# Inverse factors loaded on ScalarE's queue, first loads and last inverse in halves, and a new order, in a two-stage attention and gated spectral convolution kernel

## The chip, the cores and the metric

One core of one Trainium2 chip. The time is the device time of one execution in microseconds, the median of five runs. A profiled execution gives a page and a trace; its span runs from the first to the last instruction and is a little shorter than the time.

The engines are TensorE (PE in the profile, PEld for its weight loads), VectorE (DVE), ScalarE (ACT), GpSimd (POOL) and SyncE (SP). SP, ACT and POOL issue DMAs, each on a queue of its own.

## The reference

Eight batches, eight heads, 576 positions, head dimension 64. A packed attention makes 32 rows per head from p, k and v; a second attention lets q look at these 32 rows. The result, laid out as 576 x 512 per batch, is projected three ways; the middle third is convolved along the sequence (by Fourier transform) with a filter, gated by the other two thirds, and projected out.

```python
def sm_attn(qq, kk, vv):
    s = scale * np.matmul(qq, kk.transpose(0, 1, 3, 2))
    ...
    return np.matmul(a, vv)
p_packed = sm_attn(p, k, v)
out = sm_attn(q, p_packed, p_packed)
...
proj = x @ w_proj
x1, x2, x3 = ...
X2 = np.fft.rfft(x2, n=S, axis=1)
H = np.fft.rfft(filter_fft, n=S, axis=0)[None, :, :]
x2_conv = np.fft.irfft(X2 * H, n=S, axis=1)
y = x1 * x2_conv * x3
return (y @ w_out).astype(np.float32)
```

## The kernel before

The Fourier transforms are matrix products with constant factors: wc and wt for the forward transform, ac for the inverse. The second attention is never multiplied out: its weights a2 (per position and packed row) are transformed or transposed themselves, and the packed rows, held in R, are first multiplied with w_proj (tile wp), giving qm. So most of the work is matmuls of 16-bit tiles with 128 x 128 weights.

Each batch passes through four stages, written as generators:

- front (line 706): transposes k (k_turn, PSUM tile kTp), first scores s1 and their exponentials e1, the products with v and the sums (pv), the normalised packed rows ppn, their transpose ppT and its four copies into R (ppk in the profile), q's transposes (q_turn, copied to qT: heads 0 to 3 by VectorE, 4 to 7 by ScalarE), second scores (s2, s2t), exponentials e2 and the normalised weights a2n.
- turn (line 872): qm from R and the thirds of wp; the forward transform fp of the weights, giving fa; transposes a2tp giving a2t.
- middle (line 937): the spectrum f, multiplied by the filter's spectrum (tiles tt, gm), and the gate w from the products x1 and x3.
- back (line 1004): the inverse x2 (the matmuls `x_b<-ac,gm` in the profile, since all of x1, x2 and x3 carry the short name x_b), y as the product of gate and inverse, and five output projections o (three row groups of 128, one of mixed rows, and one, for odd batches, of the rest of two batches; tile os), each evicted and written out.

Batches 0 to 7 run as a pipeline: front of batch b beside turn of b−1, middle of b−2 and back of b−3. Ahead of it a prologue transforms the filter (hp).

Inputs are loaded by `load(b)` on POOL's queue: kn, vn and qn, cast to 16 bits on the way, in two buffers each. The first loads are those of batch 0, then the three thirds of wp, then ac, then batch 1, then wout. ac holds four factor matrices of 128 x 576; the fourth, negated values of the first two, is used for batch 0 alone (APART), whose four combinations gm aren't formed beforehand. In later batches (TURNED, KEYS, FLIP) SP turns q, k and the weights with transposing DMAs instead of PE.

The order of the instructions isn't the order of the code. A Recorder collects all operations; a planner (`schedule`) plays them through a model of engines, queues and buffers and issues, on each engine, the ready operation with the lowest priority number. The numbers are decoded from the long string PRIORITY: one shift for each of the 3168 operations. The planned order is fixed as each engine's program order. Where the planner's PE has nothing ready in the first 34 us it adds spin matmuls, whose result is unused. The planner's durations and queue constants (`hold`, `transfer_ns`, SLOW) act on the order only.

For the last batch each output projection is made in two halves of 256 columns, the first evicted by ScalarE, the second by VectorE, and half of some writes go out on ScalarE's queue.

Of the kernel before, what the change touches and what calls it, by code (L numbers as in the profile page):

```python
# [14 lines left out]
FP16 = mybir.dt.float16  # L15
# [4 lines left out]
P = 128  # L20
# [23 lines left out]
def _constants(S):  # L44
# [37 lines left out]
    ac = _f16(np.stack([*inv, np.where(COLUMN_T % 2 == 0, -inv[1], -inv[0])]).transpose(1, 0, 2))  # L82
# [4 lines left out]
    'c-oy-2RxN+8$ZuEMoLCSBqSoqmKCxq$1Ege%gPMN-Xmm0_RP)}iYVE#3W<sc8S$z&Q8?%MoPE&y`@Z+Po-^*}y6@}0{@1*3f587`q5+rudu2{1'  # L87
    '8~O8>?SK{W-z*%YoO~+%Tt%^qQ}W9U2RlaHGHLgJl$x5MTjnE|O=tXmbA`*LWsEs{+0(W2u5F=3<VZLF^xH>q4MinR3hA+#L$2=GUWVuNsrK=('
    'P?H64>q|+UKWnSXPlIHbwCnrUz3>H84Ekhorn#g_O|LykA@SxMO{a^7*i8=VRcVk5*jOEYF{Kve?CYLpb+yu2k?}gE`7^}VDcHP&v97D5g`1Jl'
    'HEm@FTSaqAEn`Dfc?Ctdq@<PvTu??*l}}Av@dCfvWmOFsEir*WO#@9axr_5UHlexow*(;f!h!>W+@!#fy-Gg%<0>f!!z{!}=7*d=(+Z4h(%UJo'  # L90
    '1TNEt^!E4kcSm<u29r?H{vsVCg}{_5XU9kHd;8=)3!dKd?TsHpO;mJ}-=kiV2Qlrj5)3!lHcNDm(BJka+r#_m*3fK8M)K@??|{Z9D#BE3G|<R>'
    '%%f|w91psiJ1H~9PFyxYn(CGmXt+7v&Gqx>Dy=VbwfWc=InKss!X#>GYohugqqXPdGFxMBRX;a3Gl{e?Z8syMtXl<>Xm#&#2iaA{KIB?iN&P}Y'
    '2B>YGW3OY{__V93Vf1IqY;D!E)|y|nl^r#GovrhgS=o(Eh2M%d8^0D8RW`jIO!)phCg(|AW{22}s`#DS53W<u&si4!Iy`LJ5<WnAejrF@;^)ET'
    'Z^x+)uJkW`9-gCsY_!NhzW)-8W^ftkQC5@sfym|ASN_RbM5ShAVCc;Tm4qCeRa$A|Qlulh5u4U23ukAtysU!svdrAH+*)KQWzA~!JioZMu!Sv;'
    'xrPPbpikFy!MpL%=h^M$)P_YlR!OFa^w5I9+Jvszg{Go`+2QwUoy(VKtWMbkSO(f8I)vE?Ojgw~Oi)p4ULc)*9r;DIac1`E(pXBAi=YCx)SOmG'
    'VysK>QUTr65Z&gF<!WvP0T#8j10&UoZ9fB2$djY{Y8qaa2-;09NlL$G`t(%sOO<rv<445^_mP1IHtMm#ul^bdoA%%k);%k|k4&DCU0jV_L4aFa'
    '_88Mqj#C0Bj*5#Mq2}j2%5(Z83zhKxgF<vHM-H7v0_^NG^ibwwl)zDFX*UJu!5;6dCF^7s1LN_%dTZ*+qAAx*`6vrRr8hDM!@|n>Ha?OMjZl+w'
    'P``zOXVv{#J}(Y#-lqP1{cCNQl@@(_jH$f2M*~ld*vAO}g!o%RXJ^LWjP?%q4ZrGZ>1*z4?s}nn?*#Y8rgCCl*2kZo9HPfs%7$vX>kZxsEN&W&'
    'Q?j0*=KR6c_;jSTx!_CGapO;RX*a5Frq~tU4+j9)*c$(yv!d;^)U=>%b65dW&h&Goj<nzk{<VGUo8D~$&CeevL8Cn?e4RaXzb8c&+`3_SQ%KX_'
    'wYIf8ZUTl_Kx!^MnH`w@{B3by#PEv4>>g6n&~RUmxZBsSy109}`iC0F_yt(`>gan$7}(r0Ft}@B?eDJPA*XNcaL32T-PXzN7mb^-tg5NlxpaXB'  # L100
    'dq-;@E0e=sj>?@S$#ta%>f4jD((=6DnQY`}`yCKZyzNuusV>39-jrKxP*T+QxY(gF!a6U*qqO>#T>mA<dvHBd7Dakt87a6P$FRPQ<29G6yEK`}'
    'hdXnt>-s;o-Eg?yDyA!GB%;f&$KcH9$ml|EIXUtG;w^RSteVG#R5^AoeFuK|3r6O9^+j)97IL?WjRKt{FH;|&<Dg)BtpJyiInTFr$5=n&Q966+'
    '^zT%aIn_zJ*Wy#UG0!R{2HJflD4iZh<;IXPbuw#D$w22MoNb;ewsg<bl$OJJM8nd(UaJdhsziuANDI&7FayeqUe>>k>S!6u;Nsa&i~O?w8TQxU'
    '%%_2tbcxFd7&Q!B|3yK~%*{YWx%W7X`Y87y%Bj<&fA1HeAZJ{lUt-+9J~lr|GR=GdgwpTRhp5ShU*g}G<X`MQl3%jfnpd@v?^jh8pYXco5?hfD'
    'MO<dEUHRsd)~LW_lhW|;3VV@R0n0a4x#cfXJL=k>S2nsO6qi?~*EbYBRF{0(o!4Urx6{&q-@X;<;cLvqB0y`Q=X+iHE~%MiW@MasSM}4xzs|=~'
    '96GjdfL3(Au47=bYpnmX#*gyO{4=RVVTlgPretd?C8R~0*@!YkBwxBj)R{Pb#8o*rJ`vV+VKVKDkpWPxpFg<fp`<IU@0qA*znfirXr)=G827lS'
    'xNXv#oBN`M^tCW4N!=@Y1xb3Ie$Jbr%Pt?>R(!hqMn`Mj&knXCm)2Gw$s0D7ju}c(9}oUMZxmoTT;I~wQW2KZ)jseo#6pw@M#5?;4-W~n_?>JY'
    'a63NBD99)EO=^8(_>B7~-|>}&!P%MOg1oaz%Emfeib`@9^$aB>IYgMX*{+*i(L5!~by-M8#++S6LHU5XxPU6>6}n3|s8#suLm4=ILNtbc3PI^t'
    'PZq|#7z+5AU*xG{yc`-*QyKK|FLEKz6tUy{ha|Zq5Bmir#7D`_P9?4lri84B-Vdutj7<=BDe$^y?W$tTMMkT3-A&d^!v9_jh3YY*JMo`%wN>QV'
    'IXh)!4>_OUmXV+zT72?_YV7xq!#XdXv=-FLBRgaN=7-4Ixmx=~O-ZM=oS5VBk&TnOz^fyhELC(VO5Y)KSW|5Cllmgd+SP_@!ptm3g-(}7D|xf$'  # L110
    'r$)^Kqsg9|qsz)yB`kQkR3qWyE;fTT=|780U#&E=(I~Rn#rv-Zw)W2Ve*Vz)PFVAC{bH|ILF!H8t4tzK!b&sB%3ZUA?1Q4cGD<4rQtt$Y=al;8'
    'hZyQ7+o;+{)kJs)KhAE*4twx2`bI|T{i)|QJu8d-tL=3HhiSjCE2tPbR`ELcTKmcB>#N@Kf@@o<b(s233r2psU)DeQYsDZ$0HFU4BVAyiI{B*J'
    '$lhvI>^Sot9&s}Z-76h#H_4#6f!6U!eK)Q&)#k(XjCn6=$nQU8c+S`RQPr85^)|;nE&-uoRpHr2QNC4t2jM0i6ZP&d?w`|Pd2cRoTFB;nTjB7i'
    '-@>Cb$2PaXr`egE6Q2Xsyw54a*#&1h7wP*|V~@q~q(}v~D>o?RD%J?{aOqSf?R!aitjI~?9{J)pIpX^(=2GZ7E2K<PK*B)P(py<w%g|F?%It=P'
    'wSl#nx=yFdg3Kx-D{X38ep_w$!jWHOqhu7DX%we*nAl#jOrEJ#?jTc<vk!dm1}<`NZEs6NbaX^?N@7e<erAwYV_E*A`*kfrg-?s@{i^H}no{Bu'
    '{gT})b9_^?eV;$ePs;PGr=-ZQdh!C%zlUwVpbDP`%PBblH99Rdg>ylU?Uj$;zb;a+S2C1V(lLX3I@!KmBlpSip1V6S`{KjNM-g>y8JcI5_d;vC'
    ')**9Ig=w+Rvbx?3_A&G~jz1a-`c~po7!@q>ab|vEkY-`A;=H1atelIZm1k4Ivu6XHZ{M~ilAg+$q^DtB-FHQtU6A`c&-{KVjbCDxfn75V!+p=v'
    '`nn4TD?+-PU$gw~%qnj$INIJ6?&DTu;U5zbnwwSERv6WCg|Sr=k&y00Q{3C07t>na&{$AkU7l-KsaO%5<J9#rH{0A)(BtNfu%Vv*rir&bjbF>F'
    'R(>O$DdKIjlB!>(KlaY8;lF2_<C1WrBD%uMNI?700TK9Q`QVc_zU7*M>l+pM*)avNArWh1+}}si?<Kldmj>T@R#N$Jo#LY2#Q>MPUVM39S2C#S'
# [1049 lines left out]
```

## Time and profile before

| | |
|---|---|
| time, median of 5 runs | 189.68 us (189.06 to 189.86) |
| profiled execution | 189.66 us, span 187.9 us |
| PE busy | 175.2 us (93%), 2477 matmuls |
| VectorE busy | 143.3 us (76%) |
| ScalarE busy | 123.5 us (66%) |
| GpSimd busy | 137.7 us (73%) |
| POOL's load queue | 17.11 MB; medians of 11.6 to 17.7 us from issue to landing |
| SP's queue | 14.59 MB |
| granted TensorE clock | 0.999 |

Almost all lines of the page name L538, the line of the Recorder that calls every recorded operation, so groups are told apart by tile names. The page's slices show PE full from the second slice to the last but one, and the DMA engines full for the first 27 of 40 slices. The batches can't be told apart by name in the page; the trace's times tell them.

### The profile page before, as it was taken

What the parts mean: (1) busy time and instruction counts of PE and PEld (TensorE: products, weight loads), DVE (VectorE), ACT (ScalarE), POOL (GpSimd) and SP (SyncE); (2) the same over time, 40 slices, a digit from 0 to 9 for tenths busy, and PEclk for the clock granted to TensorE, in tenths of its full rate; (3) what the DMA queues carried; (4) which work ended last, traced back from release to release, by engine and by line L of the source; (5) the groups of instructions that cost most, each with busy time, mean ns of one, the idle gap of its engine ahead of it and who ended that gap; (6) DMA issues with size and microseconds to landing.
All of it is one profiled execution on the core that took longest, in us unless ns stands there. A gap on an engine that the chain in (4) does not pass through costs nothing.

```text
span 187.9 us, 5930 instructions
## 1 busy us (share of the span) xinstructions
PE 175.2 (93%) x2477; PEld 117.4 (62%) x2477; DVE 143.3 (76%) x268; ACT 123.5 (66%) x261; POOL 137.7 (73%) x111
## 2 busy tenths in 40 slices
PE   0999879999989999999999999999999999999980
PEld 0447545668656767666567656757768588566770
DVE  7266889968468889987899878988766886797550
ACT  2356658698769998596964598368788844622440
POOL 7532547965698599898976998599299979979300
PEclk9999999999999999999999999999999999999999
DMA  5999999999999999999999999998762350251374
GB/s 145 289 202 197 203 203 198 265 196 203 194 218 251 199 215 192 137 167 212 198 165 249 163 126 202 155 166 231 143 191 93 112 122 3 47 177 59 127 267 112
DMA packets 52715, 32.86 MB, mean 175 GB/s; under 512 B 24592, under 2 KB 47760, under 8 KB 52688
## 3 DMA queue, kind: packets, MB, share of 16 engines
q0 software_dynamic: 29456, 17.11, 66.0%
q1 hardware_dynamic: 22576, 14.59, 36.9%
q10 hardware_dynamic: 656, 0.79, 1.7%
q8 instruction: 19, 0.31, 0.7%
q14 instruction: 8, 0.07, 0.2%
HBM read 35.39 MB, written 9.44 MB: 239 GB/s over the span
## 4 chain that ended last, share of the span: by engine, by line
PE 76%; DMA 12%; ACT 3%; DVE 3%; POOL 2%; issue 1%; DVEq 0%; POOLq 0%
PE x_b L538 26%; PE o_b L538 15%; DMA vn<-in_v_dram 9%; PE f_b L538 9%; PE hp L538 5%; PE fp_b L538 5%; PE s_b L538 4%; PE qp_b L538 3%; DMA w<-in_moe_filter_fft_dram 3%; PE pv_b L538 2%; PE kTp_b L538 2%; PE fpt_b L538 1%; PE a2tp_b L538 1%; ACT qm L538 1%; POOL qn L538 1%
## 5 line engine op out<-in xcount | busy, mean ns | idle before, releaser
L538 PE MATMUL x_b<-a2t,qm 128*128 128x64 f16 (+3 forms) x400 | 45.7, 243 | 0.0
L538 POOL TENSOR_TENSOR tt<-tt,tt 128x1024 f32<-128x1024 f32 x14 | 33.2, 2374 | 13.1 <-DVE tt L538 13.1
L538 DVE TENSOR_TENSOR tt<-f_b,h 128x1024 f32<-128x1024 f32 x32 | 38.5, 1220 | 4.7 <-PE f_b L538 3.5
L538 POOL TENSOR_TENSOR gm<-tt,tt 128x512 f16<-128x512 f32 (+1 forms) x30 | 39.6, 1350 | 0.5
L538 PE MATMUL x_b<-ac,gm 128*128 128x64 f16 (+3 forms) x300 | 38.9, 249 | 0.0
L538 PE MATMUL o_b<-wout,y 128*128 128x512 f16 (+1 forms) x144 | 35.4, 356 | 0.0
L538 ACT COPY x1s<-x_b 128x512 f32<-128x512 f32 (+1 forms) x40 | 22.0, 549 | 13.8 <-PE x_b L538 7.2
L538 PEld LDWEIGHTS <-qm 128*128 128x128 f16 x400 | 25.1, 98 | 9.3 <-issue 1.1
L538 ACT ACTIVATE os<-o_b 128x512 f32<-128x512 f32 (+1 forms) x36 | 20.4, 570 | 15.5 <-PE o_b L538 14.7
L538 DVE SCALAR_TENSOR_TENSOR y<-w,x_b 128x512 f16<-128x512 f32 x32 | 21.3, 684 | 8.7 <-PE x_b L538 8.4
L538 ACT CAST qm<-qp_b 128x512 f16<-128x512 f32 x48 | 26.1, 608 | 2.6 <-PE qp_b L538 2.4
L538 ACT ACTIVATE e<-s_b 96x384 f16<-96x384 f32 (+1 forms) x48 | 23.2, 525 | 5.8 <-PE s_b L538 5.6
L538 DVE TENSOR_TENSOR w<-x1s,x_b 128x512 f32<-128x512 f32 (+1 forms) x40 | 24.5, 629 | 2.9 <-PE x_b L538 1.9
L538 PEld LDWEIGHTS <-gm 128*128 128x128 f16 x300 | 22.2, 98 | 6.4 <-POOL gm L538 0.8
L538 PE MATMUL f_b<-qm,fa 128*128 128x512 f16 x80 | 24.7, 380 | 0.6 <-POOL fa L538 0.6
L538 POOL TENSOR_TENSOR fa<-ez 128x512 f16<-128x512 f32 x15 | 19.0, 1277 | 2.2 <-ACT ez L538 2.2
L538 PEld LDWEIGHTS <-a2n 128*128 128x128 f16 x210 | 14.0, 98 | 6.9 <-DVE a2n L538 1.7
L538 PEld LDWEIGHTS <-y 128*128 128x128 f16 x144 | 13.0, 98 | 7.1 <-issue 0.4
L538 POOL TENSOR_TENSOR a2n<-e,zr 128x1152 f16<-128x1152 f16 x7 | 15.0, 2138 | 0.6 <-DVE zr L538 0.6
L538 DVE TENSOR_REDUCE zs<-e 128x36 f32<-128x1152 f16 (+2 forms) x10 | 11.0, 1108 | 1.7 <-ACT e L538 1.7
L538 POOL DMA_DIRECT2D qn<-in_q_dram x8 | 7.2, 900 | 6.3 <-PE s_b L538 2.2
L538 ACT COPY ez<-fp_b 128x512 f32<-128x512 f32 x16 | 9.2, 588 | 3.6 <-PE fp_b L538 3.2
(82 smaller groups left out, 280.1 us busy)
## 6 DMA issues: line engine op xcount, KB each, us to landing
out_dram<-os SPq DMA_DIRECT2D x24, 256.0 KB, 2.8
kn<-in_k_dram POOLq DMA_DIRECT2D x8, 576.0 KB, 14.5
vn<-in_v_dram POOLq DMA_DIRECT2D x8, 576.0 KB, 13.2
qn<-in_q_dram POOLq DMA_DIRECT2D x8, 512.0 KB, 14.2
out_dram<-os SPq DMA_DIRECT2D x14, 128.0 KB, 2.3
wp<-in_moe_w_proj_dram POOLq DMA_DIRECT2D x3, 512.0 KB, 16.2
out_dram<-os SPq DMA_DIRECT2D x17, 64.0 KB, 2.0
w<-in_moe_filter_fft_dram SPq DMA_DIRECT2D x2, 512.0 KB, 6.3
```

Of the source, the lines that this page charges most:

```text
L538: ins = op.call(*op.args, **op.kw).ins
```

## The change

- ac loses its fourth matrix in memory and its place in POOL's queue. In turn(0), after the last copy into fa, ScalarE writes one element of ac (which ties the load to that moment), then issues the load of three matrices on its own queue, and makes the fourth itself with two negations of 288 columns each.
- kn and qn of batch 0 are loaded in two halves of four heads each.
- For the last batch the first four inverses, one per group of 128 channels over 512 positions, become four that cover two groups and 256 positions each: positions 0 to 255 of groups 0 and 1, then of 2 and 3, then positions 256 to 511 of the same. Of the latter, 32 positions belong to the even half (EVEN is 288). y is formed by one VectorE instruction for each.
- The last output projection of batch 7 is written with one DMA per batch, not one per half of the columns.
- The planner's constants change: the issue of a plain DMA from SP or ACT holds 520 rather than 440 ns; POOL transfers without a cast take 1.65 times as long; an early slow stretch of the DMA engines ends at 5500 rather than 6000 ns and is 1.7 rather than 1.6 times as slow; SP and ACT transfers start no earlier than 2000 ns; their completion takes 1300 rather than 600 ns while POOL loads are queued.
- PRIORITY is replaced: 3183 shifts.

```diff
-    ac = _f16(np.stack([*inv, np.where(COLUMN_T % 2 == 0, -inv[1], -inv[0])]).transpose(1, 0, 2))
+    ac = _f16(inv.transpose(1, 0, 2))
...
-        return 1000 + 0.45 * self.packets() if self.what == "dma_start_transpose" else 440
+        return 1000 + 0.45 * self.packets() if self.what == "dma_start_transpose" else 520
...
+        if self.engine == "POOL" and self.ins[0].dtype == self.out.dtype:
+            self.piece_ns *= 1.65
...
-    SLOW = 6000.0
+    SLOW = 5500.0
...
-        nc.gpsimd.dma_start(kn[:], k[b].rearrange("h (p i) d -> p h (i d)", i=KI))
+        for h in (slice(0, 4), slice(4, 8)) if b in (0,) else (slice(0, 8),):
+            nc.gpsimd.dma_start(kn[:, h, :], k[b, h].rearrange("h (p i) d -> p h (i d)", i=KI))
...
-        nc.gpsimd.dma_start(qn[:], q[b, :, 0:512, :].rearrange("h (p i) d -> p h (i d)", i=4))
+        for h in (slice(0, 4), slice(4, 8)) if b in (0,) else (slice(0, 8),):
+            nc.gpsimd.dma_start(qn[:, h, :], q[b, h, 0:512, :].rearrange("h (p i) d -> p h (i d)", i=4))
...
-    nc.gpsimd.dma_start(ac.rearrange("p i s -> p (i s)"), d_ac.ap()[:].rearrange("p i s -> p (i s)"))
...
+        if b == 0:
+
+            nc.scalar.copy(out=ac[0:1, 0, 0:1], in_=fa[0:1, 0, 512:513])
+            nc.scalar.dma_start(ac[:, 0:3, :].rearrange("p i s -> p (i s)"), d_ac.ap()[:].rearrange("p i s -> p (i s)"))
+            for e, c in enumerate((slice(0, EVEN), slice(EVEN, S))):
+                nc.scalar.mul(out=ac[:, 3, c], in_=ac[:, 1 - e, c], mul=-1.0)
...
-        def inverse(*ms):
+        def inverse(*ms, cols=None):
...
+            cols = cols or (slice(0, MAIN) if len(ms) == 1 else slice(MAIN, S))
+            single = cols.stop <= MAIN and b not in APART
...
-                    for c in range(split):
-                        c = ts(c, DM // split)
-                        (nc.sync, second)[u].dma_start(rows[64:128, 3, c], os_[64 * u:64 * u + 64, c])
+                    (nc.sync, second)[u].dma_start(rows[64:128, 3, :], os_[64 * u:64 * u + 64, :])
...
         for m in range(ND):
-            inverse(m)
+            if b == B - 1:
+                inverse(m % 2 * 2, m % 2 * 2 + 1, cols=slice(m // 2 * 256, m // 2 * 256 + 256))
+            else:
+                inverse(m)
```

## The prediction

> **What bounds the kernel now.** I read the table of windows first, to see where TensorE (PE) has room.
>
> ```profile
> 24.00:30.00 6.00, 4.79 (x56) 2.64 (x55) 5.27 (x13) 3.66 (x9) 3.39 (x4) 1.00 1.38 200
> 30.00:182.60 152.60, 151.90 (x2209) 104.03 (x2207) 122.34 (x212) 107.25 (x229) 122.92 (x88) 1.00 1.05 171
> 182.60:187.90 5.30, 0.00 (x0) 0.00 (x0) 0.42 (x1) 0.00 (x0) 0.00 (x0) 0.96 0.41 106
> ```
>
> After each window's length come PE, PEld, DVE, ACT and POOL busy, the granted clock, the DMA share and GB/s. Between 30 and 182.6 PE is without work for 0.7 us of 152.6. So nothing can be won in the middle except by starting it earlier, by taking matmul columns out (the change takes none out), or in the 5.3 us after the last matmul. PE busy is modelled and may hide gaps of some tens of ns, but hardly a whole microsecond.
>
> Next the chain that ended last, in order of time, at the head:
>
> ```profile
> 0.74 5.13 DMA w<-in_moe_filter_fft_dram
> ...
> 16.50 1.09 PE hp L538 x5
> 17.69 1.29 DVE h L538 x2
> 19.09 0.30 DVE ppn L538
> ...
> 20.37 1.01 ACT qT L538
> 21.41 0.27 ACT ppk L538
> 21.72 0.23 PE s2t_b L538 x2
> ...
> 25.32 0.05 issue
> 25.37 0.28 PE a2tp_b L538 x2
> ```
>
> Batch 0's first attention is a series of short steps between engines: pv, ppn, ppT, ppk, the second scores, their normalisation, and only then the transform's matmuls. PE is fed spin matmuls meanwhile (2.04 us in 18 to 24, 0.76 us in 24 to 30, by the windows of the tile spin). Two steps there wait for something that the change touches: ScalarE copies qT from 20.37 to 21.38, and the second ppk copy, which everything after needs, stands behind it.
>
> Then the loads, by the timeline of POOL and the transfer rows:
>
> ```profile
> 24.77 0.56 POOL L538 DMA_DIRECT2D ac<-c_ac  x1 [1.62 <-DMA pn_b<-in_p_dram]
> 32.44 0.79 POOL L538 DMA_DIRECT2D vn<-in_v_dram  x1
> ac<-c_ac POOLq DMA_DIRECT2D x1, 576.0 KB, 13.7
> vn<-in_v_dram POOLq DMA_DIRECT2D x1, 576.0 KB, 17.6
> ```
>
> Issue plus time to landing: ac 24.77 + 13.7 = 38.4 us, batch 2's vn 32.44 + 17.6 = 50.0 us. POOL's transfers land one after another: batch 0's kn at 12.4, vn at 15.3, qn at 18.0, the three thirds of w_proj (wp) at 22.0, 24.5 and 27.2, batch 1's kn at 30.2, vn at 33.5, qn at 36.3. The DMA digits are 9 until past 125 us. Batch 2's pv products start at 50.28, 0.25 us after their vn lands, so around 50 us the kernel goes at the pace of the loads.
>
> Last the end:
>
> ```profile
> 182.65 2.57 SPq L538 DMA_DIRECT2D out_dram<-os  x4
> 182.67 1.64 ACTq L538 DMA_DIRECT2D out_dram<-os  x3
> ```
>
> The last eviction ends at 182.63 + 0.42 = 183.05, yet SP issues until 185.2, one write each 0.6 us or so; the last, issued at 184.62, lands near 186.5.
>
> **Base.** The sums are against the profiled execution: span 187.9 us, time 189.66, so 1.76 us lie around the span. The median of the runs is 189.68; I carry differences over unchanged.
>
> **Part 1, first loads in halves (gain).** kn and qn of batch 0 become two transfers each. The queue needs 15.3 − 12.4 = 2.9 us for 576 KB, so the first half of kn lands about 1.4 us earlier, at 11.0, and the first half of qn at 18.0 − 1.35 = 16.7. Four first k transposes may start before 14.19, and pv needs vn (15.3) and the exponentials, which end at 17.42; pv starts at 17.48. At best it starts when vn is there: 17.48 − 15.3 − 0.3 = 1.9 us gained. The first q transposes may come at 16.8 and not at 19.72, so that a whole qT copy leaves the way of ppk: 21.41 − 20.1 = 1.3 us more. Upper end 3.2 us. Lower end 0: the third wp still lands at 27.2, its projection ran at 28.77, and the hp matmuls pushed back (ten, 2.2 us) need the spin slots. I take 1.2 us, nearer to the lower end, because the wp times stay. The two added issues on POOL (0.79 and 0.9 us) lie in 1.26 to 7.3, ahead of the data's arrival; vn's and qn's issues slide by 0.8 and 1.7 us but land behind kn's data anyway. POOL has had at most eight loads in flight, so the first wp is issued when one lands (10.5) instead of at 5.78; it is next in line only at 18.5. Were that cover gone, the 0.8 us of an issue would show.
>
> **Part 2, ac leaves POOL's queue.** Gain: POOL's in-order stream loses a 0.56 us issue and the 1.62 us wait before it, and the load queue loses ac's slot, 38.4 − 36.3 = 2.2 us, for all loads behind. Cost: three quarters of the bytes come back on ScalarE's queue at the same time, 0.75 × 2.2 = 1.6 us on the same DMA engines (lower bound 0.75 × 1.3 = 1.0, from the out writes below). Net +0.5 to +1.2 us for kn of batch 2 and all after, but up to 1.6 us later for what is in flight then: kn, vn and qn of batch 1. These had 1.3 us (30.2 to 31.56), 2.2 us (33.5 to 35.7) and 1.1 us (36.3 to 37.35) before PE used them. I count 0 here: it is what lets Part 1's 1.2 us survive the stage at 50 us, not an addition. For the speed of a transfer on such a queue beside loads the nearest row is the first out writes: three of 256 KB issued at 49.66 to 51.3 landed by 55.9, 6.3 us for 768 KB, some 5 us for 432 KB.
>
> A rule of the skill speaks against Parts 1 and 2. The Trainium skill, page "DMA: Bandwidth & Descriptors", section "Rules for kernel authors", says of spreading DMAs over SP, ACT and GpSimd for bandwidth that it "Doesn't help", since all run on the same 16 DMA engines and interleave, and of two halves that they serialize. The full DMA digits agree. By the rule alone both parts would be worth nothing and the forecast would be 189.4; the rows of the chain show that the order of arrival matters, not bandwidth, and I go by them.
>
> **Part 3, ScalarE's new work.** One single-element copy (0.26, the small ppk copy), one issue (0.4 to 0.55, the ACT issues at the end), two negations of 288 columns (between fa's 0.37 for 256 columns and a kT copy's 0.59 for 576; 0.4 each): 1.5 us. ACT is busy 5.45 of 6 us in 27 to 33 and 4.17 of 6 in 33 to 39; 1.8 us free there hide it. With no cover it would cost 1.5. The negations wait for ac; on ACT's queue everything planned behind them waits too: x1s, kT and e copies, and PE behind those.
>
> **Part 4, last inverse in halves.** Per m, three matmuls of 288 columns and three of 224 become three of 256, three of 32 and three of 224: twelve more matmuls in all. The spacing of 256-column ones is (2.79 − 0.27)/23 = 0.11 us, of 64-column ones (0.51 − 0.19)/11 = 0.029. So 3 × 0.11 + 3 × 0.029 against 3 × 0.123 (288/256 of the first): +0.05 per m, +0.2 us on a PE without idle. Outputs 0 and 1 can then be computed before the odd columns; with PE full that only brings their writes forward.
>
> **Part 5, the last write undivided.** Two of seven final issues go, one from SP and one from ACT. SP's last issue moves from 184.62 to some 183.85, landing 2.3 later: 186.2 against 186.5, gain 0.3. If output 2, which needs two writes on SP, is no longer the one before output 4, one more goes: landing at 185.5, gain 1.0. I take 0.5; the lower end 0.1, since the undivided write must wait for VectorE's half (183.05).
>
> **Part 6, the order.** The string is not readable by eye. In the middle it can win at most the 0.7 us; it can lose. The changed constants (hold, SLOW, shares) act only in the planner. "Late transposing DMAs" names what this profile shows no PE wait for. The waits of PE by name are 4.6 (start), 1.2, 0.6, 0.5 and 0.4 us; a new one of the larger sizes is 1.2 us. I take 0, bounds −0.7 and +1.2.
>
> **Sum.** −1.2 − 0.5 + 0.2 = −1.5 us: span 186.4, time 188.2. Its own range: best −3.2 − 1.0 − 0.7 + 0.2 = −4.7, all at once unlikely; half of each surplus above what I took gives 188.2 − 1.6 = 186.6. Worst still a gain: 189.1.
>
> **Rivals.** *Loads set the pace:* the head's gain is eaten at 50 us because vn of batch 2 comes only 0.5 us earlier or none, wp being unmoved. For it: pv 0.25 us behind its load. Against: the 2.2 us slot is gone. Then 189.7 − 0.5 + 0.2 = 189.4, chance 0.17.
>
> *The factors' transfer collides (slower):* ac is issued after fa of batch 0 (about 27 us) and meets batch 1's loads where PE has no idle. qn of batch 1 is 1.6 us later with 1.1 us of room: 0.5 us lost; if ac lands after the place where the order put the negations, ACT holds, say to 34 where 32 was planned, less its free time there, another 0.6 to 1. Decides once ac takes over some 6 us. For it: DMA is full, ACT free 1.8 us only. Against: the first use of ac was at 38.58. With the head's gain gone too: 189.7 + 0.5 + 0.8 = 191.0 less the tail's 0.3: 190.7. Chance 0.14.
>
> *The order pays for robustness:* one new wait of 1.2 us in the middle and no head gain: 189.7 + 1.2 − 0.3 = 190.6. Chance 0.11.
>
> **How the numbers follow.** A difference under 0.3% (0.57 us) can't be told from none. Forecast 0.58, 188.2. Faster 0.58, same 0.17, slower 0.14 + 0.11 = 0.25. The range, 186.3 to 190.7, cuts about a tenth at each end.
>
> **What would show it.** Right: batch 0's first a2tp at or before 24.5 (25.37 now); batch 1's qn not later than 37.3; ac landing before 35; batch 2's vn landing before 49.5; final SP issues fewer than four after the last eviction starts. Wrong: an ACT wait for DMA ac, PE idle above 1.5 us between 30 and the last matmul, or vn of batch 2 still at 50 with a2tp earlier.

## The result, and the profile after

| | before | after |
|---|---|---|
| time, median | 189.64 us (86 executions, 188.67 to 195.51) | 189.38 us (46 executions, 187.50 to 193.92) |
| ratio after to before | | 0.9966, 95% interval 0.9954 to 0.9979 |
| profiled execution | 189.66 us, span 187.9 | 191.65 us, span 189.9 |
| last matmul ends, rest of the span | 182.6, 5.3 us | 185.5, 4.4 us |

The change makes the kernel 0.34% faster by the ratio, some 0.65 us, less than half of the 1.5 us forecast; the two medians differ by 0.26 us. And it spreads the times: 10 of 46 executions took over 190.3 us (3 of 86 before), and 6 took no more than the forecast's 188.2, where before's fastest took 188.67. The ratio leaves out executions over 1.5% above a kernel's fastest, and the profiled execution is one of these, so it shows at its worst what the spread is made of.

First the table of windows of the changed kernel (after each window's length: PE, PEld, DVE, ACT and POOL busy, granted clock, DMA share, GB/s).

```profile
30.00:118.00 88.00, 87.49 (x1347) 57.38 (x1346) 73.36 (x137) 70.14 (x155) 74.68 (x57) 1.00 1.36 189
118.00:132.00 14.00, 11.09 (x205) 7.72 (x203) 9.04 (x19) 6.56 (x16) 9.17 (x7) 1.00 1.33 137
132.00:185.50 53.50, 53.50 (x686) 38.35 (x670) 40.56 (x61) 29.76 (x61) 38.09 (x24) 1.00 0.48 139
185.50:189.90 4.40, 0.00 (x1) 0.00 (x0) 0.03 (x1) 0.38 (x1) 0.00 (x0) 1.00 0.45 121
```

TensorE has nothing to do for 3.4 us between 30 us and its last matmul, where before had 0.7, and 2.9 of them lie in 118 to 132. The DMA engines are as busy there as before it, but move 137 GB/s rather than 189; before moved 193 in the same window. The waits of PE by name, in the changed kernel (us in total, times, longest):

```profile
PE s_b L543 <- DMA qT<-qn: 2.5, 1, 2.5
...
PE s_b L543 <- DMA kT<-kn: 0.4, 1, 0.4
PE x_b L543 <- DVE y L543: 0.4, 1, 0.4
```

The first is a wait that before doesn't have: batch 6's second scores wait for q's transposing DMA. In the timeline of PE of the changed kernel (start, us, what, in brackets the idle time ahead and what ended it):

```profile
127.13 0.41 PE L543 MATMUL s_b<-ppk,qT 128*128 128x64 f16 x8 [2.47 <-DMA qT<-qn]
```

SP's timeline of the same execution shows that DMA holding SP's queue for 12.85 us:

```profile
102.33 12.85 SPq L543 DMA_TRANSPOSE qT<-qn  x1
115.28 5.01 SPq L543 DMA_TRANSPOSE a2t<-a2n  x1
```

and the rows of DMA issues give their times from issue to landing (last number):

```profile
vn<-in_v_dram POOLq DMA_DIRECT2D x1, 576.0 KB, 16.1
qT<-qn SPq DMA_TRANSPOSE x1, 24.8
```

The new order issues batch 7's v load on POOL's queue at 110.97; before issued it at 115.09. Load and transposing DMA land together, at 127.05 and 127.08.

The head of the changed kernel, by the chain that ended last:

```profile
18.38 0.29 DVE ppn L543
...
19.92 0.26 ACT ppk L543
20.20 1.01 ACT qT L543
21.21 0.19 ACT e L543
21.43 0.30 DVE zs L543
...
24.84 0.70 DVE a2n L543
25.59 0.23 PE a2tp_b L543
```

ppk's last copy now comes ahead of ScalarE's copy of qT, as the forecast had it; but that copy is still in the chain, right ahead of the exponentials e, and 4.1 us of VectorE's sums, reciprocals and products (21.43 to 25.54) follow.

The factors, by ScalarE's timeline:

```profile
29.12 0.19 ACT L543 COPY ac<-fa 1x1 f16<-1x1 f16 x1
29.34 0.33 ACTq L543 DMA_DIRECT2D ac<-c_ac  x1
...
36.10 0.76 ACT L543 ACTIVATE ac<-ac 128x288 f16<-128x288 f16 x2
```

They land 5.8 us after the issue, at 35.17, and ScalarE waits for nothing there. The first inverse starts at 36.98 (38.58 before).

### The profile page after: what moved, and what is told of

The parts are those of the page before. It is cut to its first block, busy times and chain, and to the rows that moved or that the text cites. A ratio compares the mean times of both kernels' runs of the same rounds, so it can differ in the third digit from the quotient of the medians.

```text
span 189.9 us, 5963 instructions
## 1 busy us (share of the span) xinstructions
PE 176.1 (93%) x2494; PEld 117.7 (62%) x2494; DVE 143.8 (76%) x268; ACT 123.1 (65%) x264; POOL 138.1 (73%) x112
## 4 chain that ended last, share of the span: by engine, by line
PE 78%; DVE 9%; DMA 5%; ACT 3%; POOL 1%; issue 1%; ACTq 0%; DVEq 0%
PE x_b L543 27%; PE o_b L543 15%; PE f_b L543 8%; PE fp_b L543 5%; DMA kT<-kn 5%; PE s_b L543 4%; PE hp L543 4%; PE qp_b L543 3%; PE pv_b L543 3%; PE kTp_b L543 3%; DVE zs L543 2%; PE spin L543 1%; PE a2tp_b L543 1%; DVE tt L543 1%; PE qTp_b L543 1%; POOL a2n L543 1%
## 5 line engine op out<-in xcount | busy, mean ns | idle before, releaser
L543 PE MATMUL x_b<-a2t,qm 128*128 128x64 f16 (+3 forms) x400 | 46.7, 243 | 0.0
L543 PE MATMUL x_b<-ac,gm 128*128 128x64 f16 (+5 forms) x312 | 38.1, 246 | 0.4 <-DVE y L543 0.4
L543 PE MATMUL o_b<-wout,y 128*128 128x512 f16 (+1 forms) x144 | 36.2, 356 | 0.0
L543 ACT COPY x1s<-x_b 128x512 f32<-128x512 f32 (+1 forms) x40 | 21.3, 546 | 12.0 <-DVE w L543 7.0
L543 ACT ACTIVATE e<-s_b 96x384 f16<-96x384 f32 (+1 forms) x48 | 23.7, 530 | 5.8 <-PE s_b L543 5.4
L543 DVE TENSOR_REDUCE zs<-e 128x36 f32<-128x1152 f16 (+2 forms) x10 | 11.1, 1107 | 1.1 <-ACT e L543 1.1
L543 PEld LDWEIGHTS <-kT 128*128 128x128 f16 x192 | 9.0, 98 | 4.1 <-DMA kT<-kn 0.7
## 6 DMA issues: line engine op xcount, KB each, us to landing
qn<-in_q_dram POOLq DMA_DIRECT2D x7, 512.0 KB, 14.7
```

Of the source, the lines that this page charges most:

```text
L543: ins = op.call(*op.args, **op.kw).ins
```

## The experiments

In the experiments on the order, the order that the planner makes is kept and only the named instruction is moved; late_whole_inverse and the grafts below say what else they change. The edits are shown shortened, by what they do to the program. Ratios are to before, timed on the same chip, each with its 95% interval. Three or four kernels shared a chip, so ratios and not medians are compared.

Three theories stood at the start (the letters in the expectations are each run's own). A: the new order lets a load run beside a late transposing DMA, and that gives back the gain in some executions. B: the gain at the head was over-estimated. C: what was gained at all came with the last write alone.

**The changed kernel again, as the mark** (after_again).

> The changed kernel once more, for a second profile. Theory A (late transposes): the head is some 0.6 us ahead from 30 us on and the tail gives 0.5 to 1, but in most executions PE waits for a transposing DMA between 115 and 130 us, by 0 to 4 us from one execution to the next; so the times spread over 3 us or more where the kernel before spreads over 1.5, and the idle time of PE between 115 and 135 us accounts for the difference of this profile's span to 186.5. Rival B (one disturbed execution): the new profile shows no wait for qT or kT over 0.3 us, and its span is still about 187.3, so that the missing gain must be found elsewhere.

0.9992 (0.9965 to 1.0019), 188.37 to 192.19 us; 3 of 12 executions took over 190.3. Its profile is milder: batch 6's q lands at 125.0, PE hardly waits for it, but waits 0.5 us for the a2t of a later batch, again a transposing DMA. The two ratios put the worth of the change at 0.1 to 0.3%, and their intervals reach from 0.46% faster to 0.2% slower.

**Batch 7's v load issued later** (late_v7).

```diff
 def edited(nc, order):
+    move(order, "vn_b7_158", after="tt1_b4_183")      # 119.7 us rather than 111.0
```

> The changed kernel with one load moved: batch 7's v is issued on POOL some 9 us later (about 120 and not 111 us), in the same order otherwise. Theory A1 (POOL's loads for batch 7, moved earlier, slow the transposing DMA of batch 6's q, which took 24.8 us): that DMA lands before 121, the wait of 2.5 us goes, median 0.5 to 0.8 us under the changed kernel, 188.3 to 188.5. Rival A2 (the transposing DMA is slow on its own or held up behind SP's earlier k transposes and writes): it still lands at 124 to 127, time as the changed kernel's, 188.9 to 189.4. If vn of batch 7 comes too late itself: pv of batch 7 waits after 130, time over 189.5.

0.9955 (0.9936 to 0.9973), 188.36 to 189.57: the spread is gone. Rows of DMA issues of this kernel:

```profile
vn<-in_v_dram POOLq DMA_DIRECT2D x1, 576.0 KB, 8.0
...
qT<-qn SPq DMA_TRANSPOSE x1, 14.5
```

The load takes half the time it took beside the transposing DMA, and q lands at 117.2, where PE asks for it at 124.3 or later. In the four kernels with this load moved and nothing of the change undone (late_v7, and late_a2_pool, early_v7 and later_v7 below) none of 42 executions took over 190.3 us, against 10 of 46 and 3 of 12 of the changed kernel: theory A holds for the spread. But the expected 188.3 to 188.5 was not reached: the time is 0.1 to 0.2 us better than the 189.1 of the next run, which has nothing but the undivided write.

**Before with the last write undivided and nothing else** (before_one_write, and on another chip one_write_again).

```diff
-                    for c in range(split):
-                        (nc.sync, second)[u].dma_start(rows[64:128, 3, c], os_[64 * u:64 * u + 64, c])
+                    (nc.sync, second)[u].dma_start(rows[64:128, 3, :], os_[64 * u:64 * u + 64, :])
```

> The kernel before in its own order, with the one edit that the last output projection of batch 7 is written by one DMA per batch (two issues less). The prediction's Part 5: last issue on SP about 0.75 us earlier, time 0.3 us less, 189.35. Rival: the write must wait for VectorE's half and each issue starts as early as before but one, so nothing that can be told: 189.6.

> The run before_one_write once more, as the mark for the two above on this chip: before with Part 5 alone. If Part 5 carries the change's whole gain, the ratio is 0.995 to 0.998 again (0.9963 [0.9944, 0.9982] in the first job); if that was an accident of the first chip, 0.9985 to 1.001.

0.9963 (0.9944 to 0.9982) and 0.9979 (0.9962 to 0.9996). The last matmul ends at 182.4 to 182.5 (182.6 before); the rest of the span is 4.7 us rather than 5.3. The last write alone brings 0.2 to 0.4%, as much as the whole change. Theory C holds for the sum: what the rest wins and loses cancels, as the account below shows. The new order with the divided write was not run.

**First loads whole in the new order** (after_whole_loads).

```diff
-        for h in (slice(0, 4), slice(4, 8)) if b in (0,) else (slice(0, 8),):
+        for h in (slice(0, 8),):            # kn and qn of batch 0
```

> The changed kernel in its own order, but batch 0's kn and qn are loaded whole. If the halves carry the head's gain (Part 1): PE's first k transposes start at 12.6 instead of 11.2 or wait, the first a2tp comes 0.5 us or more later, time +0.4 to +0.6. Rival: the first a2tp is set by the chain through VectorE's normalisation and the wp loads, the halves give under 0.2 us, and time is unchanged.

0.9999 (0.9974 to 1.0023), against 0.9992 for the mark: no difference that can be told. Its profile fell on a mild execution: the same load, issued at 111.2, took 7.5 us and q landed at 117.1. So the same order can go either way. Its first x_b starts at 28.94, with TensorE at full speed from 8.43 (see the end); with halves it starts at 28.52 (full speed from 8.10, later_v7) and 28.70 (from 8.95, late_whole_inverse). By these, an estimate, the halves bring the head 0.3 us, which the time doesn't show.

**The factors back on POOL's queue, in the new order** (late_ac_pool: late_v7 with Parts 2 and 3 undone).

```diff
-    nc.scalar.copy(out=ac[0:1, 0, 0:1], in_=fa[0:1, 0, 512:513])
-    nc.scalar.dma_start(ac[:, 0:3, :], d_ac[:, 0:3, :])
-    nc.scalar.mul(out=ac[:, 3, c], in_=ac[:, 1 - e, c], mul=-1.0)
+    nc.gpsimd.dma_start(ac, d_ac)                      # ahead of batch 2's kn
```

> The kernel after with batch 7's v load issued late (the run before it under that name took 188.98 us, ratio 0.9955), and the inverse factors back on POOL's queue, as four matrices from memory, ahead of batch 2's k load; ScalarE's copy, issue and two negations are left out. It undoes Part 2 and Part 3 alone. Theory (the prediction's: the move is worth nothing, as the other loads are late enough anyway): ac lands at 37 to 39 us, later than the first inverse's start of 37.0, so TensorE waits up to 1 us for it there or does other work; the loads behind it land 0.5 to 1 us later and no TensorE wait follows; 188.9 to 189.3. Rival (the move was worth something: batch 1's and 2's loads come up to 1 us later and TensorE waits for them): 189.5 to 190.0. Rival (the move was a loss by ScalarE's 1.5 us ahead of the head's exponentials): 188.3 to 188.6.

1.0076 (1.0051 to 1.0101): 2.3 us dearer than late_v7, more than any theory had. The waits of PE of this kernel:

```profile
PE x_b L565 <- DMA ac<-c_ac: 1.9, 1, 1.9
```

ac lands at 39.0, and the new order has placed the first inverse at 37. The move of the factors is worth nothing by itself, but this order can't do without it.

**The last inverse in whole pieces, in the new order** (late_whole_inverse: late_v7 with Part 4 undone).

```diff
-            if b == B - 1:
-                inverse(m % 2 * 2, m % 2 * 2 + 1, cols=slice(m // 2 * 256, m // 2 * 256 + 256))
-            else:
-                inverse(m)
+            inverse(m)
```

> The kernel after with batch 7's v load late (188.98), and the last batch's inverse in whole 512-column pieces as before: Part 4 undone alone. Theory: halves cost TensorE 0.2 us of extra instructions and let the last outputs leave earlier; undone, the last matmul ends 0.1 to 0.3 us sooner, the stretch from the last matmul to the end of the span grows from 4.4 to 4.6-5.0, the time is 188.9 to 189.3. Rival (halves only cost): 188.6 to 188.8 with the same tail. Rival (halves carry the shorter tail): tail 5.2 or more, 189.5 and over.

The planner makes the order anew here; the whole pieces take the halves' priority numbers. 1.0047 (1.0029 to 1.0066), 1.7 us dearer than late_v7, where the theory had the same time. PE's timeline of this kernel near its end:

```profile
178.01 0.61 PE L566 MATMUL o_b<-wout,y 128*128 128x256 f16 x4
179.80 0.61 PE L566 MATMUL o_b<-wout,y 128*128 128x256 f16 x4 [1.18 <-DVE y L566]
```

The output projections wait 1.18 us for y, which now exists only when all the inverse's columns do. The last matmul ends 1.2 us later (183.9 against 182.75), while the rest of the span hardly changes (4.6 against 4.4). The order was made for halves, so this is their worth in this order; before, made for whole pieces, has no such wait.

**One of the head's products on POOL** (late_a2_pool: late_v7 with one 512-column a2n of batch 0 moved from VectorE).

```diff
-            nc.vector.tensor_tensor(out=a2n[...], in0=e[...], in1=zr[...], op=ALU.mult)
+            nc.gpsimd.tensor_tensor(out=a2n[...], in0=e[...], in1=zr[...], op=ALU.mult)
```

> The kernel after with batch 7's v load late (188.98), and one of batch 0's two 512-column normalising products (a2n) on POOL rather than VectorE. Theory A (with ppk earlier, the head is set by VectorE's chain of sums, reciprocals and products from 21.4 to 25.5 us, which is why Part 1 brought 0.5 us and not 1.2): the third a2n ends 0.5 to 0.7 us sooner, the first x_b starts 0.3 to 0.6 us sooner, time 188.4 to 188.7. Rival B (the third piece of wp, landing at 26.4 to 27, sets x_b's and f_b's start): x_b no sooner by over 0.15 us, time 188.9 to 189.2. Rival C (POOL's product is slow and holds up batch 2's loads queued behind it): PE waits for it, 189.2 to 190.

0.9952 (0.9934 to 0.9969), late_v7's time within a tenth of a per cent. The first x_b starts at 27.91, late_v7's at 28.72; but in this execution TensorE also came to full speed 2 us sooner, at 7.20 (see the end), which alone is worth about 1 us there: 27.80 in the run early_v7, at full speed from 7.25, which has no such product. So the profile shows no gain of the head, and the time shows none either.

**Before with batch 7's v load early** (before_early_v7).

```diff
 def edited(nc, order):
+    move(order, "vn_b7_158", after="gm_b3_131")        # 106.6 us rather than 115.1
```

> The kernel before (189.63) with only batch 7's v load issued some 7 us earlier on POOL's queue, at 107 to 108 us rather than 115, so that it runs beside batch 6's transposing q DMA, as it does in the kernel after. Theory A (the load beside it is what makes that DMA late, whatever the rest of the order): q's transposing DMA of batch 6 lands at 121 to 127 rather than 117 in the profile; TensorE, which needs it at about 124.5, waits 0 to 2.5 us; times spread upward, median 189.8 to 190.6. Rival B (the new order as a whole, or the issue time of the transposing DMA, makes it late): it lands at 117 to 119 as before, and the time stays at 189.5 to 189.7 with the old spread.

1.0010 (0.9995 to 1.0025). q's transposing DMA takes 14.7 us rather than 11.1 and lands at 120.5, just under the 121 that theory A named, and PE doesn't wait. In the ten profiles with before's order behind the head and the load later it takes 10.1 to 13.9 us, so the one early load seems to slow it in the old order as well, but there is room for it: rival B's time for theory A's reason.

**Batch 7's v load earlier still in the new order, and later still** (early_v7, later_v7).

```diff
 def edited(nc, order):
+    move(order, "vn_b7_158", after="gm_b3_131")        # early_v7: 105.1 us
...
+    move(order, "vn_b7_158", after="gm_b4_162")        # later_v7: 120.8 us
```

> The kernel after with batch 7's v load issued 6 us earlier on POOL's queue, at about 105 us rather than 111, the first moment after batch 5's products have read the buffer. It overlaps batch 6's transposing q DMA in full. Theory (a transposing DMA lands when the load beside it ends, so what counts is when the load ends): the load lands at 119 to 123, q's transposing DMA within 1 us of it, TensorE, which needs it at 124.5, doesn't wait; ratio 0.994 to 0.998. Rival (overlap itself slows the transposing DMA, the more the longer): it lands at 125 to 129, TensorE waits 1 to 4 us, ratio 1.0 to 1.012.

> As the run late_v7 (ratio 0.9955), with batch 7's v load issued one POOL product later still, so that the product which TensorE waited 0.48 us for at 121 us isn't held up by the 0.82 us of the load's issue. Theory (that wait is on the path): no wait for POOL's gm at 121 us, 0.3 to 0.5 us gained, ratio 0.9925 to 0.994. Rival (another arrival takes its place, VectorE's y or the next x_b): ratio 0.995 to 0.996.

early_v7: 0.9961 (0.9942 to 0.9980), 187.82 to 189.46. Its rows of DMA issues:

```profile
vn<-in_v_dram POOLq DMA_DIRECT2D x1, 576.0 KB, 15.6
...
qT<-qn SPq DMA_TRANSPOSE x1, 19.9
```

Load and transposing DMA land together again, at 120.6 and 121.2, early enough. later_v7: 0.9990 (0.9968 to 1.0012). Here the rival was right: the wait for POOL's gm at 121 us shrank to 0.3, and others took its place (0.4 us for kT, and 0.5 us more idle between 130 and 150). Nine of the profiles side by side, times in us; the last two columns are what POOL's queue moved while the transposing DMA was under way, and what all DMAs moved per second:

```
                    v load of batch 7   q's transposing DMA, batch 6   POOL    all
                    issued   landed     issued  landed   took          MB      GB/s
before              115.1    124.5      106.1   117.1    11.1          0.62    158
one_write_again     114.9    124.5      105.9   117.0    11.1          0.62    159
before_one_write    114.9    126.8      108.5   119.7    11.3          0.96    180
late_v7             119.7    127.7      102.7   117.2    14.5          1.49    194
before_early_v7     106.6    119.4      105.8   120.5    14.7          1.23    169
after_whole_loads   111.2    118.6      101.4   117.1    15.7          1.77    185
early_v7            105.1    120.6      101.3   121.2    19.9          2.17    177
after_again         111.6    125.1      102.0   125.0    23.0          2.10    152
after               111.0    127.1      102.3   127.1    24.8          1.93    135
```

In the five kernels whose load was issued with over 5 us to go before the transposing DMA landed, the two landed within 1.5 us of each other; in before_one_write, with 4.8 us to go, the DMA landed 7.1 us before the load. Earlier loads run beside it in every kernel, late_v7 too, whose 14.5 us have no load of v beside them. POOL's queue moves more beside it in the new order; since a longer time also lets more pass, the column alone doesn't show which causes which, but the packet counts at the end of this document do. In the two latest all DMAs also moved less per second, and no run shows why. TensorE needs q at 124.3 to 125.

**The old order behind the new head** (old_order, old_order_ac_pool; mended: graft2, graft2_ac_pool; mended again: graft3, graft3_ac_pool, graft3_a2_pool). These have Parts 1 and 5 (and, without "ac_pool", Parts 2 and 3), the head's instructions in the new order, and all others in before's.

```diff
 def edited(nc, order):
+    at = np.cumsum(np.frombuffer(zlib.decompress(base64.b85decode(ORDER)), dtype=np.int16)) - 1
+    return [order[i] for i in at]                      # the head as after, the rest as before
```

> The kernel after, with the order of before from batch 0's first projection outputs on: Parts 1, 2, 3 and 5 are in, the order after the head is the old one, and the last inverse is whole, as the old order has it (Part 4 out). Theory (the head's 0.5 us is real, and the new order gives it back in the middle through waits that the old one doesn't have): batch 6's transposing q DMA lands at 117 to 120, TensorE's losses outside the projections from 30 to 182 us are 2.5 to 3.0 us as in the run before_one_write (2.71) rather than 3.9, the last matmul ends 0.3 to 0.8 us sooner than 182.5, and the time is 0.3 to 0.8 us under before_one_write's ratio of 0.9963: ratio 0.992 to 0.9955, about 188.2 to 188.8. Rival (the head's gain ends at a later arrival whatever the order, a load or the first inverse): ratio 0.995 to 0.998 with a new wait between 35 and 60 us.

> The run old_order with the inverse factors back on POOL's queue, as four matrices, at before's place: Part 1 and Part 5 alone, without Parts 2 and 3. Theory (Part 1's head is worth nothing without Part 2, since ac lands at 38.2 to 38.5 by POOL's queue and the first inverse would be due at 38.0): TensorE waits 0.2 to 0.6 us for ac at 38 us, and the ratio is 0.001 to 0.003 above old_order's. Rival (Part 2 is worth nothing in this order): the same ratio within 0.001, no wait for ac.

1.0302 (1.0273 to 1.0331) and 1.0231 (1.0190 to 1.0273), and no evidence: the graft had put batch 1's second small q load behind its large one on POOL's queue. The waits of PE of old_order:

```profile
PE qTtp_b L598 <- DMA qt_b<-in_q_dram: 3.8, 1, 3.8
```

One load out of place by one in a queue cost 4 us and more here.

> The run old_order mended: there the graft left batch 1's second small q load behind its large one on POOL's queue, and TensorE waited 3.8 us for it, which said nothing of the question. Now POOL's loads keep before's order too, and the graft begins at batch 0's first transposed weights: Parts 1, 2, 3 and 5 with before's order behind the head. Theory (the head's gain is real, and the new order loses it again in the middle): no DMA wait at 30 to 45 us, first x_b at 29.3 to 29.6 for a clock switch at 10.2 us, TensorE's other losses from 30 to 182 us 2.5 to 3.2 us, ratio to before 0.002 to 0.004 under one_write_again's. Rival (in the old order the head's gain ends at a later arrival): within 0.001 of one_write_again or above it, with a new or longer wait in the profile between 30 and 60 us.

> The run graft2 with the factors on POOL's queue, as four matrices, at before's place: Parts 1 and 5 alone. Theory (without Part 2 the first inverse waits for ac, which lands at 38.2 to 39 us): TensorE waits 0.2 to 1.0 us for it, ratio 0.001 to 0.005 above graft2's. Rival (Part 2 is worth nothing in this order): within 0.001 of graft2, no wait for ac.

0.9966 (0.9947 to 0.9985) and 0.9967 (0.9948 to 0.9987). With and without the moved factors it is the same, and the same as the undivided write alone (0.9979 on this chip). Neither profile has a wait for ac. But this graft too had a flaw in the head: VectorE stood idle 0.58 us for an exponential that ScalarE made second and the grafted sum wanted first, as VectorE's timeline of graft2 shows:

```profile
22.99 1.28 DVE L599 TENSOR_REDUCE zs<-e 128x16 f32<-128x512 f16 x2 [0.58 <-ACT e L599]
```

> The run graft2 with one operation put right: its graft took VectorE's first sum over 512 columns from the new order and ScalarE's exponentials from the old one, so that VectorE stood idle 0.58 us at 22.4 us for the second exponential. Mended, the third a2n ends 0.4 to 0.6 us sooner than graft2's for the same clock switch, and first x_b 0.3 to 0.6 us sooner. Theory (then the head's gain comes through, since the old order has no new waits): first inverse at 38.0 to 38.3 for a clock switch at 10.2 us, last matmul 0.3 to 0.6 us sooner, ratio 0.993 to 0.995 (one_write_again 0.9979, before_one_write 0.9963). Rival (another arrival takes it up before 60 us): ratio 0.996 to 0.998, last matmul at 182.4 to 182.7 again.

> graft3 with the factors on POOL's queue as in before: Parts 1 and 5 alone with before's order behind the head. Theory (the first inverse, now due at 38.0 to 38.3, waits for ac, which lands at 38.2 to 39): TensorE waits 0.1 to 0.8 us for ac, ratio 0.0005 to 0.004 above graft3's. Rival (Part 2 is worth nothing here either): the same within 0.001.

> graft3 with one of batch 0's two 512-column normalising products on POOL, as in the run late_a2_pool, where it started the first x_b sooner and the time stayed. Theory (the head's gain comes through in the old order): first x_b another 0.3 to 0.5 us sooner than graft3's, ratio 0.001 to 0.003 under graft3's. Rival (the third piece of wp, at 26.4 to 27 us, or POOL's loads behind the product, take it up): the ratio of graft3 within 0.001 or above it.

graft3 0.9949 (0.9928 to 0.9970), graft3_ac_pool 0.9961 (0.9938 to 0.9983), graft3_a2_pool 1.0061 (1.0034 to 1.0089). graft3's last matmul ends at 182.23, 0.2 to 0.3 us before the ends of before with the undivided write alone. graft3_ac_pool does meet the wait that the theory named:

```profile
PE x_b L607 <- DMA ac<-c_ac: 0.5, 1, 0.5
```

The intervals of graft3, graft3_ac_pool and one_write_again overlap. In graft3's profile TensorE also came to full speed a microsecond sooner (9.31 against 10.35 and 10.29 of the two profiles with the write alone), which by itself moves a head by 0.5 us, and its span is no shorter (187.5 against 187.15 and 187.2). So whether the head's gain reaches the end in the old order stays open. In graft3_a2_pool the product was queued on POOL behind loads and began at 24.27, and PE paid for it:

```profile
PE a2tp_b L604 <- POOL a2n L604: 2.0, 1, 2.0
```

No version is shown to be faster than after: late_v7, late_a2_pool and graft3 have the lowest ratios, 0.9949 to 0.9955, with intervals that reach after's 0.9966. What late_v7, late_a2_pool and early_v7 do better is that their times no longer spread upward, which the ratio hardly shows, since it leaves the long executions out.

## Why the prediction was wrong

The direction was right by the ratio, and 188.2 was 1.2 us too low. Two steps failed: Part 1's gain was taken too large and followed the wrong way, and Part 6, the cost of the new order, was taken as nothing. By the prediction's own steps:

**Part 1, first loads in halves: −1.2 taken, −0.5 measured at the first x_b (some 0.3 of it by the halves, the rest by the order), and hardly anything of it in the time.** The working had two pieces. The first, pv starting up to 1.9 us sooner, came to 0.1 where it counts: at a nearly equal moment of TensorE's reaching full speed (10.35 and 10.23 us, one_write_again and after_again) the first kTp starts at 14.51 and 12.96 and the sums of pv, the prediction's 17.48, at 17.80 and 17.10, but pv's products with v at 18.19 and 18.13, because filter matmuls, scores and exponentials stand between. The second was that "a whole qT copy leaves the way of ppk: 21.41 − 20.1 = 1.3 us more". It does: the fourth ppk copy ends at 21.99 in before with one write and at 20.77 in after_again, 1.2 us sooner. But the copy went nowhere. ScalarE's timeline of one_write_again:

```profile
20.69 1.01 ACT L548 COPY qT<-qTp_b 128x1024 f16<-128x1024 f16 x1 [0.41 <-PE qTp_b L548]
21.73 0.26 ACT L548 COPY ppk<-ppT_b 64x128 f16<-64x128 f16 x1
22.29 0.28 ACT L548 ACTIVATE e<-s2t_b 128x128 f16<-128x128 f32 x1 [0.30 <-PE s2t_b L548]
```

and of after_again:

```profile
20.51 0.26 ACT L543 COPY ppk<-ppT_b 64x128 f16<-64x128 f16 x1 [0.59 <-DVE ppk L543]
20.79 1.01 ACT L543 COPY qT<-qTp_b 128x1024 f16<-128x1024 f16 x1
21.70 0.28 ACT L543 ACTIVATE e<-s2t_b 128x128 f16<-128x128 f32 x1
```

ScalarE's copy of qT starts at nearly the same time in both; only the small ppk copy has changed sides. The exponentials come 0.6 us sooner, the third a2n ends at 26.13 rather than 26.52, the first x_b starts at 29.33 rather than 29.88. What should have been asked of the step is what ScalarE, and then VectorE, do next; the prediction followed ppk and not the engine.

**Part 6, the order: 0 taken, about +0.8 to +1 and at times +3 measured.** "I take 0, bounds −0.7 and +1.2" and "Late transposing DMAs names what this profile shows no PE wait for" are where the forecast failed worst. The old profile had no such wait because its order had room for one; the new order has less. TensorE without work from 30 us to its last matmul, by the windows: 0.2 us in one_write_again, 1.05 in late_v7, 1.2 in after_again, 3.4 in after. The lines of the first three:

```profile
30.00:182.50 152.50, 152.28 (x2211) 104.03 (x2208) 122.71 (x213) 107.51 (x230) 123.12 (x89) 1.00 1.04 171
```

```profile
30.00:182.80 152.80, 151.75 (x2219) 103.67 (x2217) 122.83 (x215) 106.50 (x231) 121.92 (x87) 1.00 1.01 170
```

```profile
30.00:183.70 153.70, 152.51 (x2222) 103.63 (x2220) 123.50 (x216) 106.95 (x231) 122.05 (x87) 1.00 1.05 169
```

Where the lead goes, as TensorE's work done by a given moment, in us (worked out from the trace: each matmul counts 0.42 ns a column and 2.5 ns more, at least 27, which the spacings in unbroken rows give: eleven o_b of 512 columns in 2.54 us less the last one's 0.38 are 0.216 each, and the prediction has 0.11 and 0.029 for 256 and 64; the packed qp and pv count at their own spacing):

```
at                30    40    50    60    80    115   130   140   150   180
one_write_again   16.3  25.7  36.1  45.9  65.0   99.6 114.1 124.2 134.2 164.2
after_again       16.6  25.9  35.9  45.5  64.6   99.5 114.2 123.5 133.2 163.2
```

The head leads by 0.3 us of work at 30, the stretch from 40 to 60 takes 0.6, that from 130 to 150 another 1.1, half of it the 0.5 us wait for a2t. Then 1.0 us of work is behind, with the twelve added matmuls (0.2) to come on top: the last matmul ends at 183.66 rather than 182.44. This is Part 6's failed step: a wait that the old profile didn't have was taken as one that the new order wouldn't make. The bound of +1.2 was of the right size for one wait; that several would come, some of them in one execution and not in the next, wasn't in the sum.

**Part 5, the last write: −0.5 taken, −0.4 and −0.7 measured** (0.9979 and 0.9963 of 189.6). Right, and the only part shown to pay by itself. In the new order the rest of the span after the last matmul is 4.4 to 4.6 us rather than 5.3.

So the sum, as an estimate: −0.5 at the head, −0.7 to −0.9 at the end, +0.2 for the added matmuls and +0.8 to +1 between come to −0.4 to 0 us in the milder executions; measured were −0.26 by the medians and −0.65 by the ratio.

**Part 2, the factors' queue: 0 taken.** Right in the old order (0.9966 with, 0.9967 without). In the new order 2.3 us hang on it, since the first inverse stands ahead of where POOL's queue could bring ac; the prediction's "it is what lets Part 1's 1.2 us survive" was the right thought. The 5 us estimated for the transfer were 5.8, but by luck: the row behind the estimate was misread. The three writes issued from 49.66 us that landed by 55.9 carry 128, 64 and 64 KB, 256 together and not 768, so by that row 432 KB would have taken over 6.3 us.

**Part 3: 0 taken, right.** 1.28 us in all (0.19 + 0.33 + 0.76) against 1.5, and no wait on ScalarE.

**Part 4: +0.2 taken.** The halves add twelve matmuls, as forecast (2494 against 2482), but their price was not measured alone: in the new order the halves spare a wait of 1.18 us, in the old order that wait doesn't exist.

**The rivals.** "The order pays for robustness" had the mechanism (new waits in the middle), though with 190.6 too high a time, and a tenth of the chance. "Loads set the pace" had the number, 189.4, and not the reason: batch 2's vn landed at 48.8, 1.2 us sooner, and no wait followed. "The factors' transfer collides" didn't happen. By the rule of the Trainium skill that the prediction weighed ("DMA: Bandwidth & Descriptors", section "Rules for kernel authors", that spreading DMAs over the queues for bandwidth doesn't help), Parts 1 and 2 would be worth nothing, and the time doesn't contradict it: graft2, which has both, is 0.13% under the undivided write alone on the same chip, with intervals that overlap. The same section's row on halves is about two halves of the partitions; here the heads were halved, each half over all its partitions, and the first half of kn landed at 11.2 us rather than 12.4 (after and before).

**The signs named ahead.** Right: batch 1's qn at 36.7, batch 2's vn at 48.8, a shorter end; and the first wp was issued when a load landed, at 10.84, as Part 1 had it (in none of the twenty profiles does POOL have more than eight loads in flight). Not met: ac at 35.17 rather than before 35, the chain's a2tp at 25.59 rather than 24.5. And a sign for wrong came true in after: PE idle 3.4 us, above 1.5, between 30 and the last matmul (1.2 in after_again).

## What to carry to other kernels

An instruction moved out of one value's way is still on its engine: follow the engine to its next instruction, not only the value. A new order for a kernel whose main engine has under 1 us idle can hardly win and can easily lose, so price it at the size of the waits it may add, and look for what it lets run together (here a load beside a transposing DMA). Test the small, separable edit alone first: one write fewer at the end was worth as much as the whole change.

## What the runs showed of the hardware

**A transposing DMA beside loads.** Batch 6's q took 10.1 to 13.9 us in the old order with batch 7's v load late, 13.9 to 16.2 in the five kernels of the new order whose v load was issued only after it had landed, and 14.7 to 24.8 with that load beside it; it held SP's queue for 6.5 to 12.85 us. The packets of the two queues, by the DMA view of late_v7 from 104 to 108 us (q0 is POOL's queue, q1 SP's; packets, MB, and their time as a share of 16 engines'):

```profile
q0 software_dynamic: 828, 0.55, 90.8%
q1 hardware_dynamic: 828, 0.20, 39.3%
```

and from 116 to 117 us, when POOL's queue is empty:

```profile
q1 hardware_dynamic: 1001, 0.25, 120.0%
```

Where both queues have work they send equally many packets here, POOL's the larger; alone, SP's sends five times as many per microsecond. So a load beside the transposing DMA holds it back. The Trainium skill's page "DMA: Bandwidth & Descriptors", section "Queues, rings and completion order", has each DMA engine take turns between queues packet by packet; the equal counts agree with it. In after_whole_loads POOL's queue was all but empty from 113.3 to 115 us (16 packets against SP's 1169), and the transposing DMA was through at 117.1; in after POOL's queue kept sending until 127. Turns alone don't make after's DMA that late: from 113 to 127 us SP's queue sent 2807 packets to POOL's 1116, and all DMAs together moved 113 GB/s, where late_v7's moved 189 from 104 to 108 with both queues at work. What lowered the rate stays open. The same page's section "Rules for kernel authors" says that a transpose next to ordinary DMAs needs nothing; that stands in a row on corrupted data, and the time rose here.

**TensorE's first speed.** The filter's matmuls of 512 columns begin at 6.6 to 6.9 us and are spaced some 0.43 us until some moment, 0.216 after it, though the granted clock reads 1.00 from the start. That moment lay between 7.2 and 10.4 us in the twenty profiles. By PE's timeline, early_v7, an early one (fifteen matmuls in 3.62 us):

```profile
6.82 3.62 PE L558 MATMUL hp<-gm,wc 128*128 128x512 f16 x15
```

and one_write_again, the latest (thirteen in 4.69):

```profile
6.90 4.69 PE L548 MATMUL hp<-gm,wc 128*128 128x512 f16 x13 [0.45 <-ACT gm L548]
```

In the new order the first x_b started at 27.80 with the switch at 7.25 and at 29.33 with it at 10.23, half a microsecond for each. So heads can be compared only at equal moments; this alone moves a head by more than the change did. The Trainium skill's page "TensorE: Matmul & The Clock Gate", section "What's actually happening", puts the switch after a busy window of 3.4 us that runs free, and its variation at 0.5 us either way; here it varied by 1.6 either way.
